# Square root, edge products, second batch's folds and w2's conversions issued at other steps

## The chip, the cores and the metric

One core of one Trainium2 chip runs the whole kernel. The metric is the time of one execution on the device in microseconds (us); lower is better. The engines of the core are PE (matrix products into PSUM), DVE (vector), ACT (scalar, activations), POOL (GpSimd) and SP, which here only issues DMAs. Each engine works through its own queue of instructions; semaphores tie the queues together.

## The reference

```python
X = np.fft.fft(x, axis=1)
X = np.fft.fft(X, axis=2)
...
mu = np.mean(x, axis=-1, keepdims=True)
var = np.mean((x - mu) ** 2, axis=-1, keepdims=True)
xn = (x - mu) / np.sqrt(var + 1e-06) * g_ln
ch = np.maximum(xn @ w_ch1, 0.0) @ w_ch2
return (x + ch).astype(np.float32)
```

The input has the shape (8, 3136, 256). The real part of its two-dimensional Fourier transform is the x of the second half, a normalised network of two layers (256 to 1024 to 256) with a residual.

## The kernel before

The real part is symmetric, so only tokens 0 to 1568 of a batch are computed; a token and its mirror share their matmuls. The transform along the sequence goes in two steps. **step1** multiplies folded rows of x (sums and differences of mirrored rows, made by `fold_zw`, `fold_eo`, `fold_hi` and `fold_lo`, mostly on POOL) by a table and stores the product through SP into a scratch buffer in DRAM; `ends` and `step1_ends` do the same for the two edge columns ("edge products": three pairs of tiny matmuls on PE, copied out by ACT). **relayout** reads the scratch back turned round (tile `s2`). **step2** multiplies it by a second table into PSUM, and ACT and DVE split the result into a high and a low part (`ckh`, `ckl`), since a float32 product is made of three fp32r passes: low by high, high by low, high by high.

The network works in 49 chunks of 256 tokens (the last is longer). A chunk has eight **steps**, one for each 128 of the 1024 hidden columns; step s = 8c + f.

- `moe1_a(s)`: 6 matmuls (2 halves, 3 passes) of chunk c with w1 into PSUM `ab` (two buffers); ACT copies one half (`asb`), DVE makes sum and difference (`h`, lines 369 and 373), which frees `ab`.
- `moe1_b(s)`: ACT makes `h_hi` (ReLU, line 380), DVE `h_lo` (line 381).
- `moe2(s)`: 12 matmuls of h with w2 into `acc` (line 448).
- `residual`, `residual_e`, `residual_y`: the residual in PSUM `psy`, its mean and variance (`st`, `mv`, `ve`); the **square root** of `ve` on ACT (line 498) stands at the end of `residual_y`. `inverse_std` makes 1/std from it with four small DVE operations (lines 505 to 509), `finish` the result (lines 521 and 523), `store_out` a scatter on POOL (line 422) and row stores on SP.

The main loop issues in each step: `moe1_b(s - 1)`, `moe1_a(s)`, what `add_late` has put on step s, `moe2(s - 3)`, and what `add` has put on step s. The order on PE, ACT, DVE and POOL is the order in which this code is written (a manual schedule); so the step numbers in the `add` and `add_late` calls decide what stands behind what. In a chunk step2 falls on 8c + 5, the residual on 8c + 5 to 8c + 8, and 1/std on 8c + 9. Batch b must be ready at `need`; its steps are counted back from there. `step1_ends`, `step1` and every second step2 share one PSUM buffer, "y".

Ahead of the main loop stands a prologue, also written by hand. The weights come as float64 bit patterns and are converted by hand: `convert_a` gives `m` and `f` on DVE (lines 571 and 573) and a scaled `e` on ACT (line 579), `convert_b` edits the bits of `e` in two DVE operations (lines 584 and 586), `finish_w2` multiplies f by e on DVE (line 637), and `split_w2` makes the high part on ACT (line 590) and the low part on POOL (`w_lo`, line 591). w2 comes in four pieces, w2_0 to w2_3. Tile `f` uses the tag "f_lo", which has two buffers, so w2_0 and w2_2 share one; `e` uses the tag "zw" with three.

POOL's queue in the prologue: the three DMAs of the relayout of batch 0, the loads of batch 1, the rest of the table `tab` (line 781), the four `w_lo` of w2, then the folds of batch 1.

Of the kernel before, what the change touches and what calls it, by code (L numbers as in the profile page):

```python
# [26 lines left out]
AF = mybir.ActivationFunctionType  # L27
# [6 lines left out]
NCH = TOK // CW  # L34
# [110 lines left out]
def tile_kernel(ctx: ExitStack, tc: tile.TileContext, x, g_ln, w1, w2, tu, tab, tz, ty, tw, idx, out):  # L145
    nc = tc.nc
# [155 lines left out]
    def width(c):  # L302
        return LASTW if c == NCH - 1 else CW
# [42 lines left out]
    def hcols(c):  # L346

        return 2 * CW if width(c) == CW else LASTW + 32 + CW
# [26 lines left out]
    def moe1_b(s):  # L375
        h = hh[s]
        n = hcols(s // 8)
        h_hi = work.tile([128, n], F32R, tag="h_hi", name=f"h_hi{s}", bufs=4)
        h_lo = work.tile([128, n], F32R, tag="h_lo", name=f"h_lo{s}", bufs=4)
        nc.scalar.activation(h_hi, h, AF.Relu)  # L380
        nc.vector.scalar_tensor_tensor(out=h_lo, in0=h, scalar=0.0, in1=h_hi.bitcast(F32),  # L381
                                       op0=ALU.max, op1=ALU.subtract)
        hh[s] = (h_hi, h_lo)

    def toks(c):
        t = [(0, 0), (128, 128)]
        if width(c) > CW:
            t.append((LASTW - 32, CW))
        return t

    def tail(i):

        return i == 2
# [58 lines left out]
    res = {}  # L452
# [25 lines left out]
    def residual_y(c, i):  # L478
        ps, e, p = res.pop((c, i))
        y = work.tile([128, 258], F32, tag="ysb", name=f"y{c}_{i}", bufs=5)  # L480
        nc.vector.tensor_tensor(out=y[:p, 0:129], in0=e[:p, 0:129], in1=ps[:p, 1, 0:129], op=ALU.add)
        nc.vector.tensor_tensor(out=y[:p, 256:128:-1], in0=e[:p, 0:128], in1=ps[:p, 1, 0:128],
                                op=ALU.subtract)
        n = len(toks(c))
        if i == 0:
            stats[c] = work.tile([128, 3, 2], F32, tag="mv", name=f"mv{c}")
            if n > 2:
                nc.vector.memset(stats[c], 1.0)
        mv = stats[c]
        st = work.tile([128, 6], F32, tag="st", name=f"st{c}_{i}")  # L490
        nc.vector.bn_stats(out=st[:p], in_=y[:p, 0:D])  # L491
        nc.vector.bn_aggr(out=mv[:p, i], in_=st[:p])
        ysb[c, i] = y
        if i == n - 1:
            ve = res[c] = work.tile([128, 4, 3], F32, tag="ve", name=f"ve{c}")
            nc.vector.tensor_scalar(out=ve[:, 0, :n], in0=mv[:, :n, 1], scalar1=1e-6, scalar2=None,  # L496
                                    op0=ALU.add)
            nc.scalar.activation(ve[:, 1, :n], ve[:, 0, :n], AF.Sqrt)  # L498

    def inverse_std(c):  # L500
        n = len(toks(c))
        ve = res.pop(c)
        v, a, q = (ve[:, m, :n] for m in range(3))
        eng = nc.vector
        eng.reciprocal(q, a)  # L505
        eng.scalar_tensor_tensor(out=a, in0=q, scalar=-0.5, in1=q, op0=ALU.mult, op1=ALU.mult)
        eng.tensor_tensor(out=a, in0=a, in1=v, op=ALU.mult)
        r = rstd[c] = work.tile([128, 3], F32, tag="rstd", name=f"r{c}", bufs=3)
        eng.scalar_tensor_tensor(out=r[:, :n], in0=a, scalar=1.5, in1=q, op0=ALU.add, op1=ALU.mult)
# [42 lines left out]
    def convert_a(key, wp):  # L552
        convert_m(key, wp)
        convert_z(key, wp)
# [8 lines left out]
    def convert_m(key, wp):  # L563

        high, e = conv[key] if key in conv else convert_e(key, wp)
        low = wp.bitcast(U32).rearrange("p (n two) -> p n two", two=2)[:, :, 0]
        m = work.tile([128, 512], I32, tag="f_hi", name=f"m{key}")
        f = work.tile([128, 512], F32, tag="f_lo", name=f"f{key}")  # L570
        nc.vector.tensor_scalar(out=m, in0=high, scalar1=0xFFFFF, scalar2=0x100000,
                                op0=ALU.bitwise_and, op1=ALU.bitwise_or)
        nc.vector.scalar_tensor_tensor(out=f, in0=low, scalar=2.0 ** -32, in1=m,
                                       op0=ALU.mult, op1=ALU.add)
        conv[key] = high, e, f

    def convert_z(key, wp):
        high, e = conv[key][:2] if key in conv else convert_e(key, wp)
        nc.scalar.activation(e, high.bitcast(F32), AF.Copy, scale=2.0 ** -112)

    def convert_b(key):
        high, e, f = conv[key]
        e = e.bitcast(I32)
        nc.vector.tensor_scalar(out=e, in0=e, scalar1=3, scalar2=0x7F800000,
                                op0=ALU.logical_shift_left, op1=ALU.bitwise_and)
        nc.vector.scalar_tensor_tensor(out=e, in0=high, scalar=-0x80000000, in1=e,
                                       op0=ALU.bitwise_and, op1=ALU.bitwise_or)

    def split(hi, lo, src, eng=nc.vector):
        nc.scalar.copy(hi, src)  # L590
        eng.tensor_tensor(out=lo, in0=src, in1=hi.bitcast(F32), op=ALU.subtract)  # L591
# [4 lines left out]
    w1p, w2p = [], []  # L596
# [38 lines left out]
    def finish_w2(n):  # L635
        _, e, f = conv.pop(f"w2_{n}")
        nc.vector.scalar_tensor_tensor(out=f, in0=f, scalar=2.0 ** -20, in1=e, op0=ALU.mult,
                                       op1=ALU.mult)
        return f

    def split_w2(n, f):
        split(w2_hi[:, 2 * n:2 * n + 2], w2_lo[:, 2 * n:2 * n + 2],
              f.rearrange("p (f d) -> p f d", f=2), nc.gpsimd)
# [6 lines left out]
    def add(s, fn, *args):  # L650

        after.setdefault(s, []).append((fn, args))

    def add_late(s, fn, *args):

        late.setdefault(s, []).append((fn, args))
# [13 lines left out]
    for b in range(1, NB):  # L670
        need = 8 * (b * HALF // CW) - 3
        at = [need - d for d in ((45, 42, 37, 34, 29, 26, 21) if b > 1 else
                                 (29, 26, 23, 21, 18, 15, 13))]
        ends_at = need - (47 if b > 1 else 31)
        add(ends_at - 5, clear_x)
        add(ends_at - 5, ends, b)
        add(ends_at, step1_ends, b)
        for i, d in enumerate(at):
            add(d - 7, fold_zw, b, i, nc.gpsimd)
            add(d - 6, fold_eo, b, i)  # L680
            add(d - 4, fold_hi, b, i)
            add(d - 3, fold_lo, b, i)
            add(d, step1, b, i)
            add(d, store1, b, i)
        add(at[-1] + 2, relayout, b)
        if b + 1 < NB:
            add(at[-1] - 6, load_batch, b + 1)
    for c in range(NCH):
        n = len(toks(c))
        s = 8 * c + (5 if n == 2 else 4)  # L690
        if c == 0:
            s = 6
        for i in range(n):
            add(s + (2 if tail(i) else 0), residual, c, i)
            add_late(s + (3 if tail(i) else 1), residual_e, c, i)
            add_late(s + i + (2 if n == 2 else 1), residual_y, c, i)
            if c < NCH - 1:
                add_late(8 * c + 11 + i, finish, c, i)
                add(8 * c + 11 + i, store_out, c, i)
        add_late(8 * c + 9 + (c == 0), inverse_std, c)  # L700

    warm = work.tile([128, 2 * D], F32, tag="fold", name="warm")
    warm_r = work.tile([128, 2 * D], F32R, tag="f_hi", name="warm_r")
# [2 lines left out]
    def warm_up(n, zeros):  # L706

        pw = psum.tile([128, 2 * D], F32, tag="fft", name="pw")
        for i in range(n):
            nc.tensor.matmul(pw, zeros[:, :128], zeros, start=True, stop=True)  # L710

    E = mybir.EngineType
    with tc.manual_schedule(engines={E.PE, E.Activation, E.DVE, E.Pool}):
        with tc.manual_schedule(engines={E.SP}):
# [86 lines left out]
            f = finish_w2(0)  # L801
            split_w1(1)
            split_w2(0, f)
            convert_b("w2_1")
            warm_up(4, warm_h)
            step2(0, "m")
            step2(0, "hl")
            step2(1, "m")
            step2(1, "hl", 0)
            f = finish_w2(1)  # L810
            split_w2(1, f)
            moe1_a(0, ((1, 0), (0, 0), (0, 1)))
            step2(0, "f")
            moe1_a(1, ((1, 0), (0, 0), (0, 1)))
# [4 lines left out]
            step2(1, "f")  # L819
            step2(1, "hl", 1)  # L820
            moe2(0)
            convert_a("w2_2", w2p[2])
            moe1_b(2)
            moe1_b(3)
            moe2(1)
            step2(2, "m")
            convert_b("w2_2")
            moe1_a(4)
            f = finish_w2(2)
            split_w2(2, f)  # L830
            moe1_a(5)
            moe1_b(4)
            step2(2, "hf")
            step2(2, "l")
            moe2(2)
            convert_a("w2_3", w2p[3])
            split(t1_hi, t1_lo, tu_s[:, 0:128])
            add_late(6, convert_b, "w2_3")
            add_late(7, make_w2, 3)

        main.append(True)
        lag, last = 3, 8 * NCH
        for s in range(6, last):
# [5 lines left out]
            for fn, args in after.get(s, ()):  # L849
                fn(*args)  # L850
        moe1_b(last - 1)
        inverse_std(NCH - 1)
        for i in range(3):
            for s in range(last - lag, last):
# [21 lines left out]
```

## Time and profile before

| | us |
|---|---|
| median of 3 runs | 1054.55 |
| lowest and highest of them | 1051.33, 1055.34 |
| the profiled execution, time | 1050.93 |
| the profiled execution, first to last instruction (span) | 1049.1 |
| PE busy in the span | 1021.5 |
| DVE busy | 824.1 |
| ACT busy | 533.6 |
| POOL busy | 364.0 |
| granted PE clock, mean | 0.997 |

All times in the traces are counted in us from the start of the span. A row of a timeline gives start, length, engine, line, operation and tiles (out<-in; buffer numbers are left out); the number in brackets is the time that the engine was idle just before, and behind the arrow stands what ended that idle time. The end of a matmul is modelled, since matmuls overlap: two starts that follow each other tell the pace. A line with a stretch in front (40.20:46.00) gives how long each engine was busy in it and the granted clock of PE. When an instruction waits for several semaphores, the profile names one.

### The profile page before, as it was taken

To read this page: it belongs to the slowest core of one execution; us is meant where nothing else is said; L and a number is where in the kernel's file an instruction comes from. 1 tells how busy PE (TensorE), PEld (TensorE's weight loads), DVE (VectorE), ACT (ScalarE), POOL (GpSimd) and SP (SyncE) were. 2 spreads that over 40 slices of the span, in tenths; PEclk is the share of its full clock that TensorE was granted. 3 is DMA by queue.
4 is the path that set the end of the run, shared out by engine and by line. 5 is a ranking of instruction groups with operands and counts; after the bars stand their busy time and mean duration, and the time that the engine had idled before them with its cause. 6 is when DMAs were issued, how large, how long until landed. Compare 5 with 4: busy or idle time off the path is not lost.

```text
span 1049.1 us, 22470 instructions
## 1 busy us (share of the span) xinstructions
PE 1021.5 (97%) x8317; PEld 995.7 (95%) x8319; DVE 824.1 (79%) x2200; ACT 533.6 (51%) x1398; POOL 364.0 (35%) x456
## 2 busy tenths in 40 slices
PE   8789999999999999999999999999999999999997
PEld 5588999999999999999999999999999999999996
DVE  4888777878878778787887787877878788788885
ACT  2445544564465554555455545555555544544542
POOL 2337624550356224451255314552244501101101
PEclk9999999999999999999999999999999999999999
DMA  9921540154111720146011631128111130101101
GB/s 287 285 76 60 147 148 31 62 159 127 31 52 42 215 80 21 52 123 182 22 51 52 174 102 42 41 73 230 35 31 52 61 101 22 41 22 31 32 21 43
DMA packets 44611, 90.63 MB, mean 86 GB/s; under 512 B 6983, under 2 KB 33991, under 8 KB 43607
## 3 DMA queue, kind: packets, MB, share of 16 engines
q1 hardware_dynamic: 35063, 55.33, 18.0%
q0 software_dynamic: 8192, 32.82, 10.8%
q8 instruction: 66, 1.08, 0.4%
q10 hardware_dynamic: 1248, 1.05, 0.3%
q14 instruction: 42, 0.34, 0.1%
HBM read 48.74 MB, written 40.44 MB: 85 GB/s over the span
## 4 chain that ended last, share of the span: by engine, by line
PE 68%; DVE 13%; issue 12%; ACT 4%; POOL 2%; DMA 1%; POOLq 0%; DVEq 0%
PE acc L448 37%; PE ab L364 19%; DVE h_lo L381 5%; PE ps L318 5%; PE ps L282 3%; PE psy L467 3%; ACT h_hi L380 2%; DVE h L373 2%; DVE h L369 2%; POOL out L422 1%; DVE st L491 1%; DMA x<-x,idx 1%; ACT ckh L336 1%; PE psw L627 1%; ACT s L285 1%
## 5 line engine op out<-in xcount | busy, mean ns | idle before, releaser
L448 PE MATMUL acc<-w_hi,h_lo 128*128 128x256 f32 x1568 | 440.9, 281 | 2.8 <-DVE h_lo L381 2.6
L448 PE MATMUL acc<-w_lo,h_hi 128*128 128x256 f32 x1568 | 440.0, 281 | 1.0 <-POOL w_lo L591 1.0
L448 PE MATMUL acc<-w_hi,h_hi 128*128 128x256 f32 x1568 | 440.3, 281 | 0.0
L381 DVE SCALAR_TENSOR_TENSOR h_lo<-h,h_hi 128x512 fp32r<-128x512 f32 (+1 forms) x392 | 296.0, 755 | 181.8 <-ACT h_hi L380 180.2
L380 ACT ACTIVATE h_hi<-h 128x512 fp32r<-128x512 f32 (+1 forms) x392 | 250.1, 638 | 242.7 <-DVE h L373 242.6
L422 POOL DMA_INDIRECT out<-o,idx_s x99 | 102.2, 1032 | 579.7 <-DVE o L521 571.4
L448 PEld LDWEIGHTS acc<-w_hi,h_lo 128*128 128x128 f32 x1568 | 295.1, 188 | 3.4 <-DVE h_lo L381 3.0
L448 PEld LDWEIGHTS acc<-w_lo,h_hi 128*128 128x128 f32 x1568 | 295.9, 189 | 1.2 <-POOL w_lo L591 1.2
L448 PEld LDWEIGHTS acc<-w_hi,h_hi 128*128 128x128 f32 x1568 | 295.0, 188 | 0.0
L364 PE MATMUL ab<-ckl,w_hi 128*128 128x256 f32 x768 | 222.7, 290 | 5.3 <-DVE ve L505 2.8
L364 PE MATMUL ab<-ckh,w_lo 128*128 128x256 f32 x768 | 216.5, 282 | 0.3 <-ACT ckh L336 0.3
L364 PE MATMUL ab<-ckh,w_hi 128*128 128x256 f32 x768 | 215.7, 281 | 0.0
L369 DVE TENSOR_TENSOR h<-asb,ab 128x256 f32<-128x256 f32 x384 | 157.8, 411 | 2.7 <-ACT asb L368 2.7
L373 DVE TENSOR_TENSOR h<-asb,ab 128x256 f32<-128x256 f32 x384 | 157.7, 411 | 0.0
L364 PEld LDWEIGHTS ab<-ckl,w_hi 128*128 128x128 f32 x768 | 144.9, 189 | 11.1 <-issue 7.8
L368 ACT COPY asb<-ab 128x256 f32<-128x256 f32 x384 | 138.4, 361 | 19.1 <-PE ab L364 16.9
L364 PEld LDWEIGHTS ab<-ckh,w_lo 128*128 128x128 f32 x768 | 145.3, 189 | 2.8 <-ACT ckh L336 0.6
L364 PEld LDWEIGHTS ab<-ckh,w_hi 128*128 128x128 f32 x768 | 145.5, 189 | 0.0
L245 POOL TENSOR_TENSOR fl<-f,fh 128x512 fp32r<-128x512 f32 x49 | 63.3, 1293 | 46.7 <-ACT fh L239 45.9
L498 ACT ACTIVATE ve<-ve 128x2 f32<-128x2 f32 (+1 forms) x49 | 10.1, 206 | 135.7 <-DVE ve L496 135.7
L318 PE MATMUL ps<-tab_s,s 112*128 112x98 f32 (+1 forms) x512 | 65.7, 273 | 2.6 <-issue 2.6
L336 ACT CAST ckh<-ps 128x392 fp32r<-128x392 f32 (+49 forms) x112 | 39.5, 354 | 54.6 <-PE ps L318 54.4
(122 smaller groups left out, 1072.4 us busy)
## 6 DMA issues: line engine op xcount, KB each, us to landing
scratch<-s SPq DMA_DIRECT2D x49, 256.0 KB
s<-scratch SPq DMA_DIRECT2D x7, 1792.0 KB
x<-x SPq DMA_DIRECT2D x19, 448.0 KB
out<-o SPq DMA_DIRECT2D x154, 49.0 KB
w1p_all<-w SPq DMA_DIRECT2D x8, 512.0 KB
out<-o,idx_s POOLq DMA_INDIRECT x99, 3.5
x<-x POOLq DMA_DIRECT2D x3, 448.0 KB, 12.3
x<-x SPq DMA_DIRECT2D x6, 192.0 KB
```

The lines of the kernel that those rows point to most:

```text
L245: nc.gpsimd.tensor_tensor(out=lo, in0=f, in1=hi.bitcast(F32), op=ALU.subtract)
L282: nc.tensor.matmul(ps, (t1_hi, t1_lo)[ti], p[xi], start=(n == 0), stop=(n == 2))
L318: nc.tensor.matmul(ps[:, h, k0 - base:k1 - base], s2[b][:KP, g, 128 * h:128 * h + 128], tab_s[:, h, k0:k1], start=(h == 0 and g == 2 * j), ...
L336: nc.scalar.copy(hi, src)
L364: nc.tensor.matmul(pt, wt[wi][:, j, fs], ch[xi][:, j, :w], start=(n == 0), stop=(n == 2))
L368: nc.scalar.copy(asb[:, :w], pa)
L369: nc.vector.tensor_tensor(out=h[:, :w], in0=asb[:, :w], in1=pb, op=ALU.add)
L373: nc.vector.tensor_tensor(out=h[:, -CW:], in0=asb[:, :CW], in1=pb[:, :CW], op=ALU.subtract)
L380: nc.scalar.activation(h_hi, h, AF.Relu)
L381: nc.vector.scalar_tensor_tensor(out=h_lo, in0=h, scalar=0.0, in1=h_hi.bitcast(F32), op0=ALU.max, op1=ALU.subtract)
L422: stored(lambda: nc.gpsimd.indirect_dma_start(out, bass.IndirectOffsetOnAxis(ap=ix, axis=0), o, None), mybir.EngineType.Pool)
L448: nc.tensor.matmul(acc[c, i][:, side], hs[xi][:, h0:h0 + 128], ws[wi][:, f], start=(f == 0 and side == 0 and n == 0), stop=(f == 7 and n = ...
```

## The change

Four things are issued at other places. (1) The square root of a chunk is taken out of `residual_y`, gets a function of its own, `std`, and is issued one step later; 1/std moves a step later with it. (2) The edge products of a batch (`step1_ends`) come one step later, and the clearing and the end sums ahead of them one step earlier. (3) The folds of the second batch (b == 1) come one step earlier; its step1 and store stay. (4) In the prologue the product and split of w2_1 and all conversions of w2_2 move ahead of step2 of the first two groups, and those of w2_3 move up to where w2_2's were.

```diff
@@ -495,7 +495,10 @@
             ve = res[c] = work.tile([128, 4, 3], F32, tag="ve", name=f"ve{c}")
             nc.vector.tensor_scalar(out=ve[:, 0, :n], in0=mv[:, :n, 1], scalar1=1e-6, scalar2=None,
                                     op0=ALU.add)
-            nc.scalar.activation(ve[:, 1, :n], ve[:, 0, :n], AF.Sqrt)
+
+    def std(c):
+        n = len(toks(c))
+        nc.scalar.activation(res[c][:, 1, :n], res[c][:, 0, :n], AF.Sqrt)
 
     def inverse_std(c):
         n = len(toks(c))
@@ -671,17 +674,18 @@
         need = 8 * (b * HALF // CW) - 3
         at = [need - d for d in ((45, 42, 37, 34, 29, 26, 21) if b > 1 else
                                  (29, 26, 23, 21, 18, 15, 13))]
-        ends_at = need - (47 if b > 1 else 31)
-        add(ends_at - 5, clear_x)
-        add(ends_at - 5, ends, b)
+        ends_at = need - (46 if b > 1 else 30)
+        add(ends_at - 7, clear_x)
+        add(ends_at - 7, ends, b)
         add(ends_at, step1_ends, b)
         for i, d in enumerate(at):
+            d0, d = d, d - (b == 1)
             add(d - 7, fold_zw, b, i, nc.gpsimd)
             add(d - 6, fold_eo, b, i)
             add(d - 4, fold_hi, b, i)
             add(d - 3, fold_lo, b, i)
-            add(d, step1, b, i)
-            add(d, store1, b, i)
+            add(d0, step1, b, i)
+            add(d0, store1, b, i)
         add(at[-1] + 2, relayout, b)
         if b + 1 < NB:
             add(at[-1] - 6, load_batch, b + 1)
@@ -690,6 +694,8 @@
         s = 8 * c + (5 if n == 2 else 4)
         if c == 0:
             s = 6
+        add_late(8 * c + 9 + (c == 0), std, c)
+        add_late(8 * c + 10 + (c == 0), inverse_std, c)
         for i in range(n):
             add(s + (2 if tail(i) else 0), residual, c, i)
             add_late(s + (3 if tail(i) else 1), residual_e, c, i)
@@ -697,7 +703,6 @@
             if c < NCH - 1:
                 add_late(8 * c + 11 + i, finish, c, i)
                 add(8 * c + 11 + i, store_out, c, i)
-        add_late(8 * c + 9 + (c == 0), inverse_std, c)
 
     warm = work.tile([128, 2 * D], F32, tag="fold", name="warm")
     warm_r = work.tile([128, 2 * D], F32R, tag="f_hi", name="warm_r")
@@ -802,13 +807,15 @@
             split_w1(1)
             split_w2(0, f)
             convert_b("w2_1")
+            f = finish_w2(1)
+            split_w2(1, f)
+            convert_a("w2_2", w2p[2])
+            convert_b("w2_2")
             warm_up(4, warm_h)
             step2(0, "m")
             step2(0, "hl")
             step2(1, "m")
             step2(1, "hl", 0)
-            f = finish_w2(1)
-            split_w2(1, f)
             moe1_a(0, ((1, 0), (0, 0), (0, 1)))
             step2(0, "f")
             moe1_a(1, ((1, 0), (0, 0), (0, 1)))
@@ -819,24 +826,22 @@
             step2(1, "f")
             step2(1, "hl", 1)
             moe2(0)
-            convert_a("w2_2", w2p[2])
+            f = finish_w2(2)
+            split_w2(2, f)
             moe1_b(2)
             moe1_b(3)
             moe2(1)
             step2(2, "m")
-            convert_b("w2_2")
+            convert_a("w2_3", w2p[3])
             moe1_a(4)
-            f = finish_w2(2)
-            split_w2(2, f)
+            convert_b("w2_3")
             moe1_a(5)
             moe1_b(4)
             step2(2, "hf")
             step2(2, "l")
             moe2(2)
-            convert_a("w2_3", w2p[3])
             split(t1_hi, t1_lo, tu_s[:, 0:128])
-            add_late(6, convert_b, "w2_3")
-            add_late(7, make_w2, 3)
+            add_late(6, make_w2, 3)
 
         main.append(True)
         lag, last = 3, 8 * NCH
@@ -849,6 +854,7 @@
             for fn, args in after.get(s, ()):
                 fn(*args)
         moe1_b(last - 1)
+        std(NCH - 1)
         inverse_std(NCH - 1)
         for i in range(3):
             for s in range(last - lag, last):
```

The changed kernel's lines stand 3 further on from line 500 to 670, and 5 or more behind that: its 574, 576, 587, 589 and 640 are the old 571, 573, 584, 586 and 637, and its 594 the old 591.

Three places in the order of the instructions. The first is DVE in the prologue, between the last conversion of w2_1's e and the first h; ckl is the low part of step2's result, mw, fw and ew are m, f and e of the piece that follows in the name, and the brackets name the semaphores that are waited for. Before:

```order
L586 SCALAR_TENSOR_TENSOR ew_1_335<-w1p_all,ew_1_335 128x512 [waits DVE_49]
L340 TENSOR_TENSOR ckl_363<-ps_0_355,ckh_362 128x2x197 [waits Activation_49]
L340 TENSOR_TENSOR ckl_363<-ps_1_366,ckh_362 128x2x59 [waits Activation_49]
L637 SCALAR_TENSOR_TENSOR fw_1_337<-fw_1_337,ew_1_335 128x512 [waits DVE_49]
L369 TENSOR_TENSOR h_387<-asb_386,ab_379 128x256 [waits Activation_49]
L373 TENSOR_TENSOR h_387<-asb_386,ab_379 128x256
```

And with the change:

```order
L589 SCALAR_TENSOR_TENSOR ew_1_335<-w1p_all,ew_1_335 128x512 [waits DVE_49]
L640 SCALAR_TENSOR_TENSOR fw_1_337<-fw_1_337,ew_1_335 128x512 [waits DVE_49]
L574 TENSOR_SCALAR mw_2_354<-w1p_all 128x512 [waits DMAHW7_49]
L576 SCALAR_TENSOR_TENSOR fw_2_355<-w1p_all,mw_2_354 128x512 [waits DVE_49,Pool_49]
L587 TENSOR_SCALAR ew_2_353<-ew_2_353 128x512 [waits PE_49,Activation_49]
L589 SCALAR_TENSOR_TENSOR ew_2_353<-w1p_all,ew_2_353 128x512 [waits DVE_49]
L340 TENSOR_TENSOR ckl_374<-ps_0_366,ckh_373 128x2x197 [waits Activation_49]
L340 TENSOR_TENSOR ckl_374<-ps_1_377,ckh_373 128x2x59 [waits Activation_49]
L369 TENSOR_TENSOR h_395<-asb_394,ab_387 128x256 [waits Activation_49]
```

The product of w2_1 stood behind the two ckl and now stands ahead of them, and four operations for w2_2 have come in between; the second of them, f of w2_2, waits for POOL too.

The second place is ACT around a square root (ve), that of the third chunk, with h_hi and asb of the steps around it and a copy of step1 (s). Before:

```order
L380 ACTIVATE h_hi_1294<-h_1266 128x512
L368 COPY asb_1305<-ab_1298 128x256
L498 ACTIVATE ve_1316<-ve_1316 128x2
L285 COPY s_1_902<-ps_1_3_1331 128x4x127
L380 ACTIVATE h_hi_1342<-h_1306 128x512
L368 COPY asb_1353<-ab_1346 128x256
```

And with the change:

```order
L380 ACTIVATE h_hi_1299<-h_1271 128x512
L368 COPY asb_1310<-ab_1303 128x256
L285 COPY s_1_942<-ps_1_3_1335 128x4x127
L380 ACTIVATE h_hi_1344<-h_1311 128x512
L368 COPY asb_1355<-ab_1348 128x256
L501 ACTIVATE ve_1321<-ve_1321 128x2
L239 CAST fh_5_1373<-f_5_1296 128x512
```

The square root stood ahead of an h_hi and asb and the copy; it now stands behind them.

The third place is POOL in the second batch's first folds (zw and f of the pieces 0 to 2) against the scatters of the first chunk (out<-o). Before:

```order
L227 TENSOR_TENSOR zw_0_697<-x_80,x_81 128x256
L228 TENSOR_TENSOR zw_0_697<-x_80,x_81 128x256
L233 TENSOR_TENSOR f_0_733<-zw_0_697 128x2x128
L234 TENSOR_TENSOR f_0_733<-zw_0_697 128x2x128
L422 DMA out<-o_0_752,idx_s 25152x256
L227 TENSOR_TENSOR zw_1_807<-x_80,x_81 128x256
L228 TENSOR_TENSOR zw_1_807<-x_80,x_81 128x256
L422 DMA out<-o_1_790,idx_s 25152x256
L245 TENSOR_TENSOR fl_0_855<-f_0_733,fh_0_805 128x512
```

And with the change:

```order
L227 TENSOR_TENSOR zw_0_660<-x_80,x_81 128x256
L228 TENSOR_TENSOR zw_0_660<-x_80,x_81 128x256
L233 TENSOR_TENSOR f_0_699<-zw_0_660 128x2x128
L234 TENSOR_TENSOR f_0_699<-zw_0_660 128x2x128
L227 TENSOR_TENSOR zw_1_771<-x_80,x_81 128x256
L228 TENSOR_TENSOR zw_1_771<-x_80,x_81 128x256
L422 DMA out<-o_0_752,idx_s 25152x256
L245 TENSOR_TENSOR fl_0_810<-f_0_699,fh_0_769 128x512
L233 TENSOR_TENSOR f_1_812<-zw_1_771 128x2x128
L234 TENSOR_TENSOR f_1_812<-zw_1_771 128x2x128
L422 DMA out<-o_1_795,idx_s 25152x256
```

The sums zw of the second piece have moved ahead of the first scatter, and the first low part fl and the second f ahead of the second scatter.

## The prediction

> **What bounds the kernel now.** I read the page first, then a table of windows by stage, then the list of TensorE's waits, and then the timelines of the stages that still have idle time.
>
> ```profile
> PE 1021.5 (97%) x8317; PEld 995.7 (95%) x8319; DVE 824.1 (79%) x2200; ACT 533.6 (51%) x1398; POOL 364.0 (35%) x456
> core 0: us, PE busy (x) PEld busy (x) DVE busy (x) ACT busy (x) POOL busy (x), PEclk, DMA share, GB/s
> 40.20:46.00 5.80, 5.29 (x31) 4.88 (x31) 2.20 (x5) 2.29 (x6) 1.81 (x3) 0.71 1.03 240
> 46.00:75.00 29.00, 23.78 (x186) 22.33 (x187) 25.26 (x56) 14.29 (x38) 9.76 (x12) 1.00 0.47 130
> 75.00:120.00 45.00, 41.48 (x337) 40.26 (x336) 35.38 (x87) 23.82 (x64) 31.29 (x35) 1.00 0.18 55
> 120.00:1030.00 910.00, 905.64 (x7555) 896.89 (x7554) 726.70 (x1973) 478.14 (x1261) 305.25 (x376) 1.00 0.27 78
> ```
>
> PE is the bound: from 120 to 1030 us it is idle for 4.4 us of 910. The change takes no matmul away, so it can only win idle time: 5.2 us between 46 and 75, 3.5 between 75 and 120, those 4.4, and a little at the end. Between 46 and 75 DVE is busy for 25.3 of 29 us; there DVE sets the pace and PE waits for it. After 120 DVE has slack in every step.
>
> **The conversions of w2.** In the old order DVE waits here:
>
> ```profile
> 35.20 0.42 DVE L571 TENSOR_SCALAR mw<-w1p_all 128x512 int32<-128x512 int32 x1
> 35.65 0.69 DVE L573 SCALAR_TENSOR_TENSOR fw<-w1p_all,mw 128x512 f32<-128x512 uint32 x1
> 36.26 0.68 DVE L637 SCALAR_TENSOR_TENSOR fw<-fw,ew 128x512 f32<-128x512 f32 x1
> 38.51 0.69 DVE L586 SCALAR_TENSOR_TENSOR ew<-w1p_all,ew 128x512 int32<-128x512 int32 x1
> 42.13 0.57 DVE L340 TENSOR_TENSOR ckl<-ps,ckh 128x394 fp32r<-128x394 f32 x1 [2.92 <-ACT ckh L336]
> ```
>
> By the starts of these rows a 0.42 op takes 0.45 until the next and a 0.69 op 0.61. The change puts five such ops ahead of the ckl of 42.13: the product of w2_1, then m, f and the two edits of e for w2_2, together 0.61 + 0.45 + 0.61 + 0.45 + 0.61 = 2.7 us, into a wait of 2.92 us. By size they fit.
>
> But f of w2_2 takes the "f_lo" tag, which has two buffers, and w2_0 and w2_1 hold both. It gets w2_0's buffer, so it must wait until POOL has made w_lo of w2_0; the order shows that wait on Pool. POOL is late there:
>
> ```profile
> 46.16 0.70 POOL L781 DMA_DIRECT2D tab_s<-tab  x1 [2.85 <-DMA s<-scratch]
> 46.88 2.52 POOL L591 TENSOR_TENSOR w_lo<-fw,w_hi 128x512 fp32r<-128x512 f32 x2
> 46.92 3.04 DVE L381 SCALAR_TENSOR_TENSOR h_lo<-h,h_hi 128x512 fp32r<-128x512 f32 x1
> 46.96 0.38 ACT L368 COPY asb<-ab 128x256 f32<-128x256 f32 x1 [0.21 <-PE ab L364]
> 49.88 0.41 DVE L369 TENSOR_TENSOR h<-asb,ab 128x256 f32<-128x256 f32 x1
> ```
>
> POOL issues the rest of tab only when the third piece of the relayout has landed, and the two w_lo stand behind that issue: the first runs from 46.88 to about 48.15 (half of 2.52). No DVE instruction stands ahead of that landing, so the change does not move it. Before, f of w2_2 came only after the fourth moe1_a, when the buffer was free. Now DVE has done the product and m by about 40.2 and stands until 48.2, with e and both ckl queued behind. (w2_2's load was issued well ahead; up to 48 even a late landing would cost nothing, as POOL ends later. The same holds for ACT's part of e.) DVE doesn't pass over an instruction that waits: the h at 49.88 had its asb at 47.34 and still came after the h_lo that was held.
>
> Next, f is let go while POOL is in the second w_lo, until 49.40. No row shows this form beside a POOL op. The nearest is the h_lo at 46.92, also SCALAR_TENSOR_TENSOR of two SBUF tiles with 512 elements: it ended at 49.96, 0.56 after POOL, instead of after 0.69. I take the same for f: end 49.96. Then e twice (start 49.88, 50.32), ckl at 50.93 and 51.42, the second done at 51.7: PE gets it at **51.8**. If f isn't held, 1.1 us earlier, 50.7. (The Trainium skill, page "SBUF — State Buffer", section "Who interferes with whom", says that a DVE instruction with two SBUF inputs contends with a GpSimd instruction that reads SBUF, and that whichever issued first keeps the port for its whole length. The held h_lo agrees: 0.56 after POOL's end. By that rule f is held too and the sum stays; without it the sum below is 1.1 us lower.)
>
> ```profile
> 40.24 0.66 PE L318 MATMUL ps<-tab_s,s 112*128 112x99 f32 x4 [2.63 <-issue]
> 43.53 0.41 PE L364 MATMUL ab<-ckl,w_hi 128*128 128x256 f32 x1
> 43.74 0.41 PE L364 MATMUL ab<-ckh,w_lo 128*128 128x256 f32 x1
> 46.24 0.28 PE L364 MATMUL ab<-ckh,w_hi 128*128 128x256 f32 x1
> 46.36 0.28 PE L364 MATMUL ab<-ckl,w_hi 128*128 128x256 f32 x1
> ```
>
> The matmul of 43.53, the first that needs ckl, starts at 51.8: PE is **8.3 us late** there. Its clock was 0.71 in 40.2 to 46 after an idle of 2.63 (pace 0.21, then 0.12); after an idle of 8 I expect the slow pace again for some 3 to 7 us. I price that at nothing more: DVE's chain after the restart is longer than the matmuls even at 0.21.
>
> How much is caught up by 75? These are PE's waits of the old run:
>
> ```profile
> 47.15 0.35 PE L364 MATMUL ab<-ckl,w_hi 128*128 128x256 f32 x1 [0.28 <-DVE h L373]
> 50.01 0.39 PE L448 MATMUL acc<-w_hi,h_lo 128*128 128x256 f32 x1 [1.92 <-DVE h_lo L381]
> 62.77 0.36 PE L364 MATMUL ab<-ckl,w_hi 128*128 128x256 f32 x1 [0.77 <-DVE h L373]
> 66.26 0.38 PE L448 MATMUL acc<-w_hi,h_lo 128*128 128x256 f32 x1 [0.22 <-ACT w_hi L590]
> 67.61 0.38 PE L448 MATMUL acc<-w_lo,h_hi 128*128 128x256 f32 x1 [0.97 <-POOL w_lo L591]
> 74.72 0.36 PE L364 MATMUL ab<-ckl,w_hi 128*128 128x256 f32 x1 [1.07 <-DVE ve L505]
> ```
>
> Their sum is 5.2, so between nothing and 5.2 is caught up, and the lag at 75 lies between 8.3 and 3.1. I laid DVE's rows behind one another in the new order with these durations. The wait of 1.92 goes (POOL is done, h_lo takes 0.69), w2_3's w_lo is early enough for 67.61, and the sqrt no longer stands ahead of h_hi at 74.72. New waits take some back: about 1.0 for the seventh moe1_a, since DVE now makes m and f of w2_3 ahead of the h that frees its PSUM; about 0.8 for the tenth, since w_lo of w2_3 holds h_lo 1.3 us and the POOL folds follow at once; 0.3 in small ones. So 5.2 − 2.1 = 3.1 is caught up: **+5.2** at 75.
>
> **The square root.**
>
> ```profile
> 87.22 3.31 DVE L381 SCALAR_TENSOR_TENSOR h_lo<-h,h_hi 128x512 fp32r<-128x512 f32 x1
> 91.34 0.35 PE L364 MATMUL ab<-ckl,w_hi 128*128 128x256 f32 x1 [0.51 <-DVE h L373]
> 92.50 0.20 ACT L498 ACTIVATE ve<-ve 128x2 f32<-128x2 f32 x1 [5.35 <-DVE ve L496]
> 93.74 0.69 DVE L381 SCALAR_TENSOR_TENSOR h_lo<-h,h_hi 128x512 fp32r<-128x512 f32 x1 [1.27 <-ACT h_hi L380]
> 95.24 0.36 PE L364 MATMUL ab<-ckl,w_hi 128*128 128x256 f32 x1 [1.55 <-DVE ve L505]
> 118.56 0.27 PE L448 MATMUL acc<-w_hi,h_hi 128*128 128x256 f32 x1
> 118.96 0.36 PE L364 MATMUL ab<-ckl,w_hi 128*128 128x256 f32 x1
> 827.20 0.28 PE L448 MATMUL acc<-w_hi,h_hi 128*128 128x256 f32 x1
> 827.59 0.36 PE L364 MATMUL ab<-ckl,w_hi 128*128 128x256 f32 x1
> 1037.97 0.39 PE L448 MATMUL acc<-w_hi,h_lo 128*128 128x256 f32 x1 [0.70 <-DVE h_lo L381]
> ```
>
> ACT takes its queue in order: the sqrt waits for ve, the next h_hi behind it, and DVE idles 1.27 us before h_lo. PE pays only where it has no lead. (The row names ve L505, but the h that frees PE's PSUM ended just before it.) One step later ve is long there and nothing waits. That takes 1.55 at 95.24, and 0.51 at 91.34 where DVE's lead was eaten: −2.1. At the same place of later chunks PE's start is 0.40 after the last one instead of 0.12 (118.56 to 118.96; 0.39 at 827.20, the last). In 22 of the 45 chunks from 118.96 to 1001 the surplus is over 0.02 us; read off one by one it sums to −3.0. At the end 0.70 goes: −0.7. The sqrt still runs 49 times at 0.20 on an ACT that is 51% busy, and 1/std comes a step later, at 8c+10, ahead of the finish at 8c+11.
>
> **Edge products and folds.**
>
> ```profile
> 108.71 0.47 PE L282 MATMUL ps<-fl,t_hi 128*128 128x512 f32 x1 [1.33 <-DVE ckl L340]
> 171.72 0.36 PE L257 MATMUL pse<-e0c,tu_s 128*128 128x14 f32 x2 [1.19 <-DVE ckl L340]
> 776.63 0.36 PE L257 MATMUL pse<-e0c,tu_s 128*128 128x14 f32 x2 [1.14 <-DVE ckl L340]
> ```
>
> The edge products share the one PSUM buffer "y" with a step2 and were issued in the step in which DVE frees it. A step later it is free: −2.3. The step1 of 108.71 waits for the same and isn't moved: 0. The clearing and end sums a step earlier stand at the same place of POOL's queue for later batches: 0. The second batch's folds a step up move POOL's chain against the scatters; DVE is held somewhere else: 0, with −1.3 and +2.6 as ends (108.71 gone; one more hold like 87.22, 3.31 instead of 0.69). SP's stores swap places five times, with nobody waiting: 0.
>
> **The sum**, on the profiled execution (span 1049.1, time 1050.93): +5.2 − 2.1 − 3.0 − 0.7 − 2.3 = −2.9, so 1048.0. The median of the three runs shown is 1054.55, 0.34% above; on that scale the forecast is **1051.6**. 0.5% is about what a measurement of this kernel can tell from no change, 5.3 us.
>
> **The rivals.**
>
> 1. *f doesn't wait, and the change does what it says.* Then ckl comes 0.2 us late, PE not at all, and 46 to 75 gains 0.77 + 0.22 + 0.97 + 1.07 = 3.0 (the 1.92 stays, as POOL's w_lo still meets h_lo). −3.0 − 8.1 = −11.1: 1043.4. For it: the five ops fit in 2.92. Against it: the wait on Pool in the order. Chance 0.08.
> 2. *The lag is caught up nearly whole*: f isn't held (−1.1) and all of 5.2 is won back. +2.0 − 8.1 = −6.1: 1048.4. DVE has five operations on w2 less to do after the restart, and 3.7 of the 29 us were idle before. Chance 0.17.
> 3. *POOL's folds hold DVE while it has no lead.* A step up and with PE late, the chain of folds of the second batch meets h_lo again and again up to 120, at 3.31 − 0.69 = 2.6 each. In the old run PE paid 0.51 for one. Without a lead it pays all: from the second the change is slower than before, +2.3 (1056.9), with three +4.9 (1059.5). For it: POOL is busy 31.3 of 45 us there. Against: PE lost only 3.5 us there in all, in spite of it. Chance 0.13, half of it over the bound.
>
> **How the numbers follow.** The forecast has 0.62, from −6 to 0 by the two open steps (1.1 of f, 2.1 of new waits). Faster by over 0.5%: all of rival 1, most of 2 and a little of the forecast, 0.26. Slower: 0.06. Within: 0.68. The range takes in rivals 1 to 3 but for the third hold: 1043.5 to 1057.5.
>
> **What would show it.** Right: DVE idle for some 8 us ahead of f (line 576), ended by POOL w_lo; PE idle for about 8 us ahead of ab, ended by ckl; no idle on ACT ahead of the sqrt and none of PE at the edge products; from 120 to 1030 PE idle under 1.5 us. Wrong: ckl near 42.3, or PE's clock low well past 60, or a new wait in every chunk.

## The result, and the profile after

| | us |
|---|---|
| before, median of 7 runs | 1052.34 |
| lowest and highest of them | 1050.77, 1055.34 |
| after, median of 7 runs | 1046.05 |
| lowest and highest of them | 1044.66, 1050.27 |
| after, the profiled execution, time | 1050.27 |
| after, its span | 1048.1 |

The ratio is 0.9948, with a 95% interval of 0.9935 to 0.9962: 5.5 us faster (4.0 to 6.8), half a per cent, against the 2.9 that the prediction summed up; the two medians themselves lie 6.3 apart. Below, the gains in us are the ratio's, and the time of a kernel is its median. The profiled execution of after was the longest of its seven, and the reason lies ahead of the change: its first step2 matmul, which waits for the relayout, started at 44.92 instead of 40.24, and at 40.59 when the same kernel was profiled once more (after_again). So I count both traces from that matmul.

From the page and the table of windows of after (stages cut some 6 us later than before, since the relayout landed later and PE stood longer):

```profile
PE 1020.9 (97%) x8319; PEld 996.3 (95%) x8319; DVE 826.4 (79%) x2200; ACT 538.4 (51%) x1398; POOL 365.6 (35%) x456
46.00:52.00 6.00, 1.94 (x13) 1.48 (x11) 0.00 (x0) 1.14 (x3) 2.08 (x3) 0.62 1.02 238
52.00:82.00 30.00, 23.99 (x176) 23.01 (x176) 23.03 (x48) 13.23 (x35) 10.36 (x13) 0.85 0.42 114
82.00:126.00 44.00, 42.08 (x339) 40.70 (x338) 37.27 (x91) 24.32 (x65) 28.73 (x32) 1.00 0.17 52
126.00:1030.00 904.00, 903.74 (x7572) 897.49 (x7571) 730.46 (x1980) 483.87 (x1263) 307.80 (x377) 1.00 0.27 78
```

From 126 to 1030 PE is idle for 0.26 us of 904, where it was 4.4 of 910. The price stands in the first two rows: from 46 to 52 DVE does nothing at all. The list of PE's waits of after (us in total, times, longest) and the timeline of the place say why:

```profile
PE ab L364 <- DVE ckl L340: 8.2, 1, 8.2
PE ab L364 <- DVE h L373: 1.8, 4, 0.8
PE ps L282 <- DVE ckl L340: 1.5, 1, 1.5
44.58 0.69 DVE L640 SCALAR_TENSOR_TENSOR fw<-fw,ew 128x512 f32<-128x512 f32 x1
45.19 0.42 DVE L574 TENSOR_SCALAR mw<-w1p_all 128x512 int32<-128x512 int32 x1
50.92 0.70 POOL L786 DMA_DIRECT2D tab_s<-tab  x1 [2.76 <-DMA s<-scratch]
51.64 2.50 POOL L594 TENSOR_TENSOR w_lo<-fw,w_hi 128x512 fp32r<-128x512 f32 x2
52.95 1.74 DVE L576 SCALAR_TENSOR_TENSOR fw<-w1p_all,mw 128x512 f32<-128x512 uint32 x1 [7.34 <-POOL w_lo L594]
54.62 0.41 DVE L587 TENSOR_SCALAR ew<-ew 128x512 int32<-128x512 int32 x1
55.07 0.69 DVE L589 SCALAR_TENSOR_TENSOR ew<-w1p_all,ew 128x512 int32<-128x512 int32 x1
55.68 0.75 DVE L340 TENSOR_TENSOR ckl<-ps,ckh 128x394 fp32r<-128x394 f32 x2
56.48 0.58 PE L364 MATMUL ab<-ckl,w_hi 128*128 128x256 f32 x1 [8.20 <-DVE ckl L340]
```

Read it from the top. DVE has finished m of w2_2 at 45.61 and stands for 7.34 us before f, until POOL has done its first w_lo; POOL did not begin, since the DMA issue ahead of it waited for the relayout's third piece. The two ckl stand behind f on DVE, and PE behind ckl. The waits on ve, on h_lo, on w_lo and at the edge products (pse) that the list of before had are gone.

To see where the time comes and goes I use the start of the twelve matmuls of moe2(s), counted from the first step2 matmul, and take the same number of before off it. The first column is the first matmul that reads ckl.

| us against before | ckl | s = 9 | 24 | 43 | 44 | 283 | 284 | 380 | 391 |
|---|---|---|---|---|---|---|---|---|---|
| after | 8.28 | 5.50 | 3.48 | 3.21 | 1.13 | -1.65 | -3.68 | -3.82 | -5.69 |
| after_again | 7.93 | 5.15 | 3.13 | 2.84 | 0.76 | -2.02 | -4.04 | -4.19 | -6.04 |
| prologue_only | 7.94 | 5.52 | 5.12 | 5.10 | 5.48 | 6.59 | 6.57 | 6.58 | 6.58 |
| tab_sp | 4.90 | 2.10 | 0.06 | -0.23 | -2.31 | -5.09 | -7.12 | -7.26 | -9.13 |
| no_prologue | 0.54 | -1.31 | -3.33 | -3.62 | -5.70 | -8.48 | -10.50 | -10.65 | -12.50 |
| third_f | -0.01 | -1.56 | -3.63 | -3.91 | -5.99 | -8.77 | -10.80 | -10.94 | -12.82 |
| sqrt_only | 0.93 | -1.18 | -2.89 | -3.17 | -3.30 | -6.67 | -6.74 | -7.53 | -9.35 |
| edges_only | 1.38 | -0.09 | -2.07 | -2.09 | -4.17 | -1.32 | -3.35 | -2.27 | -2.31 |
| folds_only | 0.03 | -0.09 | 0.54 | 0.50 | 0.48 | 0.52 | 0.52 | 0.52 | 0.53 |
| both | 1.68 | -1.86 | -3.93 | -4.21 | -6.30 | -9.07 | -11.10 | -11.25 | -13.08 |
| pe_warm | 8.52 | 4.49 | 2.44 | 2.17 | 0.08 | -2.69 | -4.72 | -4.87 | -6.73 |
| third_f_nofolds | 0.40 | -0.78 | -1.98 | -2.26 | -4.35 | -7.12 | -9.15 | -9.30 | -11.13 |

Row by row, after: 8.28 lost at the restart, 2.78 of it caught up by step 9, 2.0 won up to step 24, then two drops of 2 us at the edge products of the third and the last batch (steps 43 and 283), a slow slide in between, and 1.9 won from step 380 on. The other rows belong to the experiments.

### The profile page after: what moved, and what is told of

Same layout as the page of the kernel before. It is cut to its first block, busy times and chain, and to the rows that moved or that the text cites. A ratio compares the mean times of both kernels' runs of the same rounds, so it can differ in the third digit from the quotient of the medians.

```text
span 1048.1 us, 22494 instructions
## 1 busy us (share of the span) xinstructions
PE 1020.9 (97%) x8319; PEld 996.3 (95%) x8319; DVE 826.4 (79%) x2200; ACT 538.4 (51%) x1398; POOL 365.6 (35%) x456
## 4 chain that ended last, share of the span: by engine, by line
PE 77%; issue 12%; DVE 4%; POOL 2%; DMA 1%; ACT 1%; POOLq 0%; DVEq 0%; ACTq 0%
PE acc L448 43%; PE ab L364 22%; PE ps L318 4%; PE psy L467 3%; PE ps L282 3%; POOL out L422 1%; DVE h_lo L381 1%; DMA s<-scratch 1%; DVE h L369 1%; DVE h L373 1%; ACT h_hi L380 0%; DVE ckl L340 0%; DVE st L491 0%; POOL spacer L406 0%; ACT ckh L336 0%
## 5 line engine op out<-in xcount | busy, mean ns | idle before, releaser
L422 POOL DMA_INDIRECT out<-o,idx_s x99 | 99.4, 1004 | 547.6 <-DVE o L524 539.2
L285 ACT COPY s<-ps 128x508 f32<-128x508 f32 x56 | 32.8, 585 | 87.6 <-PE ps L282 66.4
```

The source lines that it names most:

```text
L285: nc.scalar.copy(s[:, :, :, :127], ps[:, :, :, :127])
L422: stored(lambda: nc.gpsimd.indirect_dma_start(out, bass.IndirectOffsetOnAxis(ap=ix, axis=0), o, None), mybir.EngineType.Pool)
```

## The experiments

My theory: the change holds a gain of some 9 to 11 us in its first three parts, and part 4 gives about 5 back through one wait, f of w2_2 on POOL. The rivals: the stall is caught up anyway and the gain was small; or the clock after the stall, or the folds, carry a part of it.

### Part 4 alone, and the change without it

Kernel prologue_only is before with the last hunks of the diff, from `split_w1(1)` on; no_prologue is after with those undone:

```diff
             convert_b("w2_1")
-            f = finish_w2(1)
-            split_w2(1, f)
-            convert_a("w2_2", w2p[2])
-            convert_b("w2_2")
             warm_up(4, warm_h)
...
             step2(1, "hl", 0)
+            f = finish_w2(1)
+            split_w2(1, f)
...
```

> The kernel before with part 4 alone (the conversions of w2 in the prologue moved); square root, edge products and folds stay. My theory: f of w2_2 waits for POOL's w_lo of w2_0, PE stands about 8.2 us ahead of the first ab that reads ckl, and some 3 of these are caught up by the twelfth step: 4 to 6 us slower than before, a ratio near 1.005. Rival (the lag is caught up nearly whole, or part 4 is no loss): within 2 us of before. The trace is to show PE ab <- DVE ckl near 8.2 and DVE f held by POOL w_lo near 7.3.

> The change without part 4: square root, edge products and folds as changed, the conversions of w2 as before. My theory: the stall of 8 us is gone and all gains stay: 10 to 12 us faster than before, a ratio near 0.989, and 5 to 6 us faster than the whole change. Rival (what is left after the twelfth step is not the prologue's): about as fast as the whole change, 5 us faster than before.

Measured: prologue_only 1057.43, ratio 1.0051 (1.0039 to 1.0063), 5.4 us slower than before; no_prologue 1040.13, ratio 0.9892 (0.9876 to 0.9907), 11.4 faster. The two multiply to 0.9942, and after has 0.9948: the stall and the gains add up. The timeline of prologue_only shows the stall without any other part of the change:

```profile
48.19 1.75 DVE L573 SCALAR_TENSOR_TENSOR fw<-w1p_all,mw 128x512 f32<-128x512 uint32 x1 [7.69 <-POOL w_lo L591]
51.72 0.58 PE L364 MATMUL ab<-ckl,w_hi 128*128 128x256 f32 x1 [6.85 <-DVE ckl L340]
```

The idle of 7.69 before f and the 6.85 of PE behind it are the step that the prediction named. In the table it is 7.94 at the restart and 5.52 at step 9, and that never comes back. (The further 1.0 of this row, just behind step 44, is not the stall's: in this trace PE's clock stood at 0.50 for 3.4 us from 178.0 on, which the other traces don't have there.)

### The wait itself: taken away, and shortened

third_f gives f of w2_2 a buffer of its own, so that nothing of w2_0 has to be done first. tab_sp leaves the buffer and moves the DMA that POOL stood at ahead of w_lo.

```diff
-        f = work.tile([128, 512], F32, tag="f_lo", name=f"f{key}")
+        f = work.tile([128, 512], F32, tag="f_c" if key == "w2_2" else "f_lo", name=f"f{key}",
+                      bufs=1 if key == "w2_2" else 2)
```

```diff
-            nc.gpsimd.dma_start(tab_s[:, :, gb[8]:], tab[:, :, gb[8]:])
...
             nc.sync.dma_start(idx_s, idx)
+            nc.sync.dma_start(tab_s[:, :, gb[8]:], tab[:, :, gb[8]:])
```

> The changed kernel with one edit: f of w2_2 has a buffer of its own, so it needs no w_lo of w2_0 to be done. My theory: the wait on POOL was the whole fault of part 4; DVE does the five operations while it waited for the relayout, PE gets ckl within 0.5 us of before, and the time is 10 to 14 us under before (ratio 0.987 to 0.990), as fast as the change without part 4 or up to 3 us faster. Rival A (DVE or PE is slowed by something else in this order): no faster than the change without part 4, or slower. Rival B (the wait is not what costs): the same as the whole change.

> The changed kernel with the rest of the table tab loaded by a DMA that SP issues and no longer POOL, so that POOL's w_lo of w2_0 no longer stands behind the landing of the relayout's third piece but behind POOL's own issues ahead of it. My theory: f of w2_2 is let go earlier by as much as w_lo starts earlier, some 2.8 us or more (the 2.76 that POOL stood for that landing), and PE's wait for ckl goes from 8.2 to 5.5 us or less; with about 60 per cent of that kept, 1.5 to 3 us faster than the whole change, so about 7 to 8 under before. Rival (PE's lag does not carry through): same time as the whole change.

Measured: third_f 1039.14, ratio 0.9872 (0.9858 to 0.9886), 13.5 us under before; tab_sp 1044.74, ratio 0.9935 (0.9918 to 0.9952), 6.8 under before. The timelines of third_f (first three rows) and of tab_sp (the others):

```profile
41.10 0.42 DVE L575 TENSOR_SCALAR mw<-w1p_all 128x512 int32<-128x512 int32 x1
41.55 0.69 DVE L577 SCALAR_TENSOR_TENSOR fw<-w1p_all,mw 128x512 f32<-128x512 uint32 x1
43.53 0.95 DVE L340 TENSOR_TENSOR ckl<-ps,ckh 128x394 fp32r<-128x394 f32 x2
...
45.36 2.52 POOL L594 TENSOR_TENSOR w_lo<-fw,w_hi 128x512 fp32r<-128x512 f32 x2
46.68 1.75 DVE L576 SCALAR_TENSOR_TENSOR fw<-w1p_all,mw 128x512 f32<-128x512 uint32 x1 [6.68 <-POOL w_lo L594]
50.22 0.58 PE L364 MATMUL ab<-ckl,w_hi 128*128 128x256 f32 x1 [2.91 <-DVE ckl L340]
```

With a buffer of its own f follows m at once, takes 0.69 instead of 1.74, and all five operations lie in DVE's wait for the relayout; PE gets ckl as early as before (-0.01 in the table). That is the whole fault of part 4, and the edit gives the fastest kernel of the study. Part 4 without the fault brings little: third_f ends 0.3 us ahead of no_prologue in the traces, and the intervals of the two overlap.

tab_sp is the same fault at another dose. w_lo comes earlier, PE's lag at the restart is 4.90 instead of 8.28, and all of these 3.4 are still there at the end (-9.13 against -5.69). My expectation that 60% would carry through was wrong: the part that is caught up by step 9 is 2.80 here and 2.78 in after and in after_again, the same at both doses and not a share. Of the 3.4 the ratios show 1.3 against after and nothing against after_again, which is 7.5 under before; the edit has a price of its own. These are the DMA rows for two pieces of the relayout (KB, median us from issue to landing), of tab_sp and of after:

```profile
s<-scratch POOLq DMA_DIRECT2D x2, 448.0 KB, 8.9
...
s<-scratch POOLq DMA_DIRECT2D x2, 448.0 KB, 5.0
```

With the table's load among the transfers that run then, the relayout lands later. From POOL's issue of it to the first step2 matmul it takes 7.5 us in tab_sp (34.51 to 42.03) and 5.0 in after (39.88 to 44.92); in the other kernels whose table is loaded by POOL it takes 4.8 to 5.8.

### Both repairs together

> The changed kernel with both repairs: a buffer of its own for f of w2_2, and the rest of tab loaded by SP, so that POOL's w_lo of w2_0 and w2_1 run about 1.5 us earlier. My theory: PE's wait for the h_lo that the second w_lo holds, 1.5 us when only the buffer is added, shrinks to under 0.5; the time is 0 to 1.5 us under the one with the buffer alone, that is 13 to 15 us under before. Rival (w_lo a little earlier holds another DVE operation just as long): no gain or a loss of up to 1 us against the buffer alone.

Measured: 1041.43, ratio 0.9904 (0.9892 to 0.9917): slower than third_f with its 0.9872, and by more than the rival allowed, so the expectation failed. Its first half held: PE's wait of 1.5 for h_lo, which the second w_lo held in third_f, is gone from the list of waits, though only 0.3 us of it is left at step 9 (-1.86 against -1.56). But the relayout takes 7.6 us from its issue to the first step2 matmul, as in tab_sp, and 4.9 in third_f. The 2.7 lost there less the 0.3 is 2.4. Against the before beside each, the medians of the two differ by 2.9 and the ratios by 3.4, so this is most of the loss; the table, which starts behind the relayout, has both 0.3 ahead of third_f to the end.

### The other three parts, one by one

Each is before with one part of the diff: the new function `std` and its three calls; the two lines of `ends_at` and what follows them; the line with `d0`.

```diff
+            d0, d = d, d - (b == 1)
...
-            add(d, step1, b, i)
-            add(d, store1, b, i)
+            add(d0, step1, b, i)
+            add(d0, store1, b, i)
```

> The kernel before with part 1 alone (square root and 1/std a step later). By the terms of my prediction 2.1 + 3.0 + 0.7 = 5.8 us faster. By the starts of the twelve-matmul steps in the trace of the whole change (3.8 from step 48 to 380, 1.9 in the last twelve, 2 up to step 16) it is 7 to 8 us faster, since an idle figure leaves out a part of what lies between two starts. Rival (the gain of the whole change came from the folds): under 3 us faster.

> The kernel before with part 2 alone (edge products a step later, clearing and end sums a step earlier). By the idle figures of my prediction 2.3 us faster, by the starts of the steps 3.5 us; no wait of PE pse on DVE ckl is left. Rival (the wait moves to the next user of the buffer y): no change.

> The kernel before with part 3 alone (the second batch's folds a step earlier). My theory: no change, between 1.3 us faster and 2.6 slower; the step1 wait near 108 us stays at about 1.3. Rival (a fold holds DVE where it has no lead): a new PE wait of 1 to 3 us between 75 and 120, slower by as much.

| | median | ratio (95%) | us against before |
|---|---|---|---|
| sqrt_only | 1042.12 | 0.9917 (0.9898 to 0.9937) | -8.7 |
| edges_only | 1049.96 | 0.9990 (0.9980 to 1.0000) | -1.1 |
| folds_only | 1053.55 | 1.0016 (1.0002 to 1.0029) | +1.7 |

**The square root** is the change's gain. The prediction had 5.8 for it, by idle figures. Where the rest lies can be read from two pieces of PE's timeline at the same square root: of before (first row; the two matmuls ahead of it start at 827.20 and 827.59, in rows of the prediction) and of sqrt_only (the others).

```profile
827.78 0.28 PE L364 MATMUL ab<-ckh,w_lo 128*128 128x256 f32 x1
...
819.91 0.28 PE L448 MATMUL acc<-w_hi,h_hi 128*128 128x256 f32 x1
820.03 0.28 PE L364 MATMUL ab<-ckl,w_hi 128*128 128x256 f32 x1
820.15 0.28 PE L364 MATMUL ab<-ckh,w_lo 128*128 128x256 f32 x1
```

The start at 827.59 is late by 0.39 - 0.12 = 0.27, which I had counted, and the matmul behind it starts 0.19 after it instead of 0.12, which I had not: the step loses 0.34. In the 22 chunks that the prediction summed, this second part is 1.6 in all. Summed over the steps 24 to 380, sqrt_only wins 4.6 where the prediction had 3.0, so it is the whole difference. The other shortfall is the end:

```profile
1019.40 0.39 PE L364 MATMUL bb<-ckl,w_hi 128*128 128x264 f32 x1 [1.19 <-DVE h L373]
...
1010.85 0.39 PE L364 MATMUL bb<-ckl,w_hi 128*128 128x264 f32 x1 [0.28 <-DVE h L373]
```

The first row is before, the second sqrt_only: 0.9 of the wait was the square root's too, and I had left that row out. With the h_lo wait (0.70 by its idle figure, 0.85 from start to start) the end gives 1.8, not 0.7.

**The edge products** lose their waits as expected: -2.08 from step 43 to 44 and -2.03 from 283 to 284, of which 0.63 each is the six small matmuls' own time that moves on one step, so 2.85. Alone they give most of it back: edges_only wins another 2.0 up to step 24, and still it ends at -2.3 in its trace and at -1.1 by the ratio, where I had expected 2.3 to 3.5. The timelines of edges_only (first three rows) and of before (the others) at the square root of the same chunk:

```profile
175.81 0.21 ACT L498 ACTIVATE ve<-ve 128x2 f32<-128x2 f32 x1 [3.19 <-DVE ve L496]
177.92 0.28 PE L448 MATMUL acc<-w_hi,h_hi 128*128 128x256 f32 x1
178.55 0.36 PE L364 MATMUL ab<-ckl,w_hi 128*128 128x256 f32 x1 [0.36 <-DVE ve L505]
...
181.52 0.27 PE L448 MATMUL acc<-w_hi,h_hi 128*128 128x256 f32 x1
181.69 0.36 PE L364 MATMUL ab<-ckl,w_hi 128*128 128x256 f32 x1
```

The same matmul starts 0.63 after the one ahead of it instead of 0.17. That is 0.45 in each of six chunks, 2.7 in all: with the edge products a step nearer, the old square root costs PE more. When the square root moves as well, these 0.45 don't appear (no_prologue and sqrt_only have the same step there). So the two parts are worth more together than apart. Why the nearness costs 0.45 wasn't taken apart.

**The folds** alone cost about 1.7 (0.2 to 3.1). In PE's timeline of folds_only one wait has grown:

```profile
120.69 0.36 PE L364 MATMUL ab<-ckl,w_hi 128*128 128x256 f32 x1 [1.25 <-DVE ve L505]
```

In before the same place has 0.13 (118.96). It is again the h behind the square root, so it should go when the root does; the next runs ask that. The trace ends only 0.5 behind before: it loses 1.1 at that place and wins 0.7 earlier, since the wait of 0.51 that before has at 91.34 is not there.

### The clock after the stall, and the folds in company

pe_warm fills PE's 8 us with 30 matmuls of zeros, so that its clock is up when ckl comes; third_f_nofolds is third_f with the folds at their old step; after_again is the changed kernel beside them.

```diff
             step2(1, "hl", 0)
+            warm_up(30, warm_h, "acc1")
             moe1_a(0, ((1, 0), (0, 0), (0, 1)))
```

```diff
-            d0, d = d, d - (b == 1)
+            d0 = d
```

> The changed kernel with 30 matmuls of zeros put on PE ahead of the first moe1_a, in the 8 us in which PE stands for ckl, so that its clock is not lowered when ckl comes. My theory: the lower clock after the stall costs nothing, since DVE's chain sets the pace there: same time as the whole change run beside it, within 1 us. Rival: the slow 5 us behind the restart cost 1.5 to 3 us, and this kernel is faster by as much.

> The changed kernel once more, as the neighbour of the other two on the same chip: 5 to 6 us under before, ratio 0.994 to 0.996.

> The changed kernel with a buffer of its own for f of w2_2, and the second batch's folds back at their old step. If the folds cost 1.7 us in this company as they did alone, it is 1 to 2 us under the one with the buffer and the folds a step up (ratio 0.985 to 0.987). If what they cost alone was paid at the square root, which is gone here, it is the same, 0.986 to 0.988, with no PE wait near 120 us in either.

Measured: pe_warm 1045.35, ratio 0.9936 (0.9913 to 0.9958); after_again 1045.55, ratio 0.9929 (0.9912 to 0.9946); third_f_nofolds 1039.78, ratio 0.9875 (0.9853 to 0.9896). That is a little better for after_again than I had expected (0.994 to 0.996). The windows behind the restart, of after (three rows) and pe_warm (two):

```profile
56.00:58.00 2.00, 1.52 (x7) 1.52 (x8) 0.43 (x2) 0.26 (x1) 0.00 (x0) 0.50 0.97 196
58.00:60.00 2.00, 1.94 (x9) 1.68 (x9) 1.32 (x4) 1.41 (x4) 0.00 (x0) 0.50 0.99 233
60.00:62.00 2.00, 2.00 (x15) 2.00 (x14) 1.62 (x5) 1.21 (x4) 0.00 (x0) 0.74 1.04 390
...
52.00:54.00 2.00, 1.58 (x13) 1.37 (x11) 0.68 (x2) 1.08 (x3) 0.00 (x0) 1.00 1.00 217
54.00:56.00 2.00, 1.78 (x15) 1.81 (x16) 1.80 (x5) 1.38 (x3) 0.00 (x0) 1.00 0.98 316
```

In after the clock is at 0.50 for some 4.6 us from the restart at 56.48; in pe_warm, which reads ckl at 52.24, it is at 1.00 at once. The medians are the same, as I had expected, but an interval of 0.9913 to 0.9958 could hide a us or two. The traces show a small price: pe_warm reads ckl 0.2 to 0.6 later than after and after_again, and yet at step 9 it stands 0.7 to 1.0 ahead of them (4.49 against 5.15 and 5.50), which it keeps to the end. My reason was wrong, too: between 58 and 60 PE at half speed is busy for 1.94 of 2 us and DVE for 1.32, so there PE sets the pace; at full speed PE is busy for 1.58 and 1.78 and waits for DVE. So the clock is a small part of the loss, not none.

The folds change nothing in this company that the medians can tell (0.9875 against 0.9872, measured on two chips). The traces can tell a little. These are rows of third_f_nofolds (two) and of sqrt_only, which doesn't move the folds either:

```profile
90.55 3.31 DVE L381 SCALAR_TENSOR_TENSOR h_lo<-h,h_hi 128x512 fp32r<-128x512 f32 x1
94.66 0.36 PE L364 MATMUL ab<-ckl,w_hi 128*128 128x256 f32 x1 [1.31 <-DVE h L373]
...
90.27 0.35 PE L364 MATMUL ab<-ckl,w_hi 128*128 128x256 f32 x1 [0.69 <-DVE h L373]
```

It is the h_lo held for 3.31 and the wait behind it that before has at 87.22 and 91.34. In third_f, with the folds a step up, POOL holds an h_lo for 2.21 at 79.93 and another for 2.13 at 99.94, and PE waits behind neither; neither kernel has the wait at 120. From step 9 to 24 third_f wins 2.07 and third_f_nofolds 1.20. So in this company the step up wins some 0.9 in the trace, where alone it loses 0.6 over the same steps: it moves the places where POOL holds DVE, and which of them are paid depends on the rest of the order.

## Why the prediction was right or wrong, point by point

- **f waits for POOL: right.** Predicted were 8 us of idle on DVE, f held by the second w_lo to 0.56 after POOL's end, and PE 8.3 late. The trace has 7.34, an end at 54.69 with POOL's at 54.14, and 8.28. third_f showed by taking the wait away that nothing else was in it. The Trainium skill, page "SBUF — State Buffer", section "Who interferes with whom", has a DVE instruction with two SBUF inputs contend with a GpSimd instruction that reads SBUF; f agrees, at 1.74 us beside w_lo and 0.69 in third_f without it.
- **3.1 caught up, +5.2 left: right, with some luck.** 2.78 and +5.5. The new waits before the seventh and tenth moe1_a came as 0.81 and 0.63 (predicted 1.0 and 0.8), all new waits together as 1.8 instead of 2.1; the clock, priced at nothing, took some 0.7 to 1.0. The two misses offset each other in part.
- **The clock at nothing: nearly right in size, wrong in its reason.** The medians show no difference, the traces 0.7 to 1.0 us. DVE's chain was not the longer one while the clock was at 0.50.
- **2.1 up to step 24: right in size**, 2.0 in after. That it was the square root alone was wrong. The wait of 0.51 at 91.34 is not its own: sqrt_only still has 0.69 there (90.27), and edges_only and folds_only, which leave the root where it was, have none. Of the 1.55 at 95.24 sqrt_only keeps 0.27 (92.91), but edges_only, too, keeps only 0.35 (93.11), and it wins 2.0 between steps 9 and 24. There the second batch's edge products, clearing and end sums move, and I had put those at 0; which of them does it wasn't taken apart. The parts remove the same waits.
- **The steady part of the square root, 3.0: too small.** It was 4.6. The mechanism was right; the term counted the late matmul and not the one behind it, which is late by another 0.07.
- **The end, 0.7: too small.** It was 1.9 in after; the wait at 1019.40 belonged to the square root and was not in the sum.
- **The edge products, 2.3: nearly right**, 2.85 from start to start; but only with the square root moved.
- **The folds at 0: inside the bounds given.** Alone they cost 1.7 by the ratio; beside third_f's other parts the medians show nothing and the traces a gain of some 0.9. That DVE is held somewhere else is what the rows of third_f show, and that its holds are shorter and not paid there. In the changed kernel itself they were not taken out.
- **The sum.** The forecast was -2.9, the ratio has -5.5 and the trace -5.7. The terms that were too small make it up: 1.6 (steady) + 1.2 (end) + 0.5 (edges) - 0.3 (stall) = 3.0. The time of 1046.05 lies within the range; of its 5.5 below the 1051.6 forecast 2.2 are due to the median of before, 1054.55 of three runs and 1052.34 of seven. The forecast was no measurable change; the result lies just past the 0.5% bound, and the same kernel run again had 0.9929. The prediction's first rival, the change without the stall, is what third_f became: 13.5 under before, where the rival had 11.1 with the same small terms.

## What to carry to other kernels

When work moves into an idle stretch, its durations say whether it fits, and its semaphores say whether it may start there: look up who must release each buffer that it takes, and what that engine's queue is waiting for. Price a wait on the bound engine from start to start, the next instruction included, and not by the idle figure alone. Try the parts of a change apart and together, since a part that loses alone can be free, and one that wins can be worth nothing, depending on whose slack it uses.

## What the runs showed of the hardware

- A matmul that has waited delays the one behind it too: starts of 0.39 and 0.19 us where both were 0.12 (827.20 to 827.78 in before, 819.91 to 820.15 in sqrt_only), though the second shows no idle.
- PE's clock stayed at 0.50 for some 4.6 us of nearly full work after the stall of 8.2 us, in after, with PE as the bound; 30 matmuls of zeros in the stall kept it at 1.00 and won 0.7 to 1.0 us in the traces, too little for the medians (1045.35 against 1045.55). The Trainium skill, page "TensorE: Matmul & The Clock Gate", section "Part 1: The HAM clock gate", gives about 3.4 us of sustained work until the clock is up; the traces have 3.4 (prologue_only, from 51.7 to 55.1) to 4.6 here.
- A load of 686 KB put among the relayout's transfers came with a later landing of the relayout: 7.5 us from its issue to the first step2 matmul in tab_sp and 7.6 in both, against 4.8 to 5.8 in the eleven other traces, though SP had issued the one and POOL the other.
